# A GLU that works on feature pairs, with its 64-row remainders as two row tiles, inside a statically scheduled four-layer kernel

## The chip, the cores and the metric

One core of one Trainium2 chip. Times are microseconds (us) on the device. In this kernel TensorE does the matmuls and writes their sums to the banks of PSUM, a memory of its own; the vector engine (DVE) and the scalar engine (ACT) read them out (the evacuation), and GpSimd (POOL) does elementwise work on SBUF, the main on-chip memory. "Span" is the time from the first to the last instruction of a profiled run. In profile lines PE is TensorE's matmuls, PEld its weight loads, and L1076 is line 1076 of the kernel that ran. "A row tile" is half of the TensorE array, 64 of its 128 rows, used as an array of its own.

## The reference, cut to what matters

Two blocks A (linear attention) and two blocks B (a gated bilinear unit, GLU) alternate over 2048 tokens of width 576; each adds to x.

```
x = x + A(layernorm(x));  x = x + B(layernorm(x))      # twice

def B(x):                     # D = 576, F = 4608
    g = x @ w_gate            # [2048, 4608]
    u = x @ w_up
    return (g * u) @ w_down
```

The contraction over D = 576 is 4 chunks of 128 rows and a remainder of 64.

## The kernel before: the parts that matter

The order of instructions on each engine is fixed when the kernel is built. The kernel carries a list scheduler: each piece of work is a Python generator (a "thread") that yields groups of instructions with planned durations; the scheduler always takes the group that could start first in its plan. The GLU thread `t_bmain` has priority 10, and priority 10 has a head start ("bias") of 300 ns:

```python
SEM_LAT = 64.0                                  # planned cost of a semaphore, ns
self.bias = {10: 300.0}
...
    est = max(self.free_at[eng], tr.ready_time(deps), th.t_ready)
    key = (est - self.bias.get(int(th.prio), 0.0), -th.prio)
    if best is None or key < best[0]:
        best = (key, th, est)
```

The GLU thread, for a block b of 256 tokens and a feature tile f of 128 (cut):

```python
for i in range(total + LAG):                    # LAG = 2
    b, f = divmod(i, NF)
    if f == 0:
        yield ("wait", ("xTB", L, b))           # attention and layernorm of this block done
    gub = s.GU_BANKS[i % 2]                     # two PSUM banks alternate
    # 5 gate matmuls -> columns 0:256 of the bank, 5 up matmuls -> columns 256:512;
    # the fifth of each is the remainder, 128 rows padded with zeros
    yield ("ops", "pe", ops)
    yield ("ops", "act", [Op(372, copy gate half of the bank -> gsb)])
    yield ("ops", "dve", [Op(425, up half of the bank * gsb -> hT)])
    # then the down matmuls of tile i - LAG: 2 x (512 + 64 columns)
```

While the second half of a layer's attention still runs, its threads (projection, softmax, transposes, output projection for each of 16 token tiles) compete with the GLU thread for TensorE.

Of the kernel before, what the change touches and what calls it, by code (L numbers as in the profile page):

```python
# [424 lines left out]
def d_pe(n):  # L425
    return max(n, 64) / 2.4 + (7.0 if 288 <= n < 512 else 3.0)
# [18 lines left out]
class K:  # L445
# [19 lines left out]
    def alloc(self):  # L465
        nc = self.nc
        A = lambda name, shape, dt: self.stack.enter_context(nc.sbuf_tensor(name, shape, dt))
        self.ident = A("ident", [128, 128], BF16)
        self.onesf = A("onesf", [128, 128], F32)
        self.epst = A("epst", [128, 1], F32)  # L470
        self.mask = A("mask", [TW, TW], BF16)
        self.ind = A("ind", [TW, HT], BF16)
        self.BDphi = A("BDphi", [TW, NT, TW], BF16)
        self.BD = A("BD", [TW, 2 * NT, 114], BF16)
        self.x_sb = A("x_sb", [128, NS, D], BF16)
        self.xT = A("xT", [128, 6, S], BF16)
        self.Wq = A("Wq", [128, 4, D], BF16)
        self.Wqr = A("Wqr", [128, 288], BF16)
        self.Wk = A("Wk", [128, 4, D], BF16)
        self.Wkr = A("Wkr", [128, 288], BF16)  # L480
        self.Wv = A("Wv", [128, 4, DP], BF16)
        self.Wvr = A("Wvr", [128, 324], BF16)
        self.Wo = A("Wo", [128, 4, D], BF16)
        self.Wor = A("Wor", [128, 288], BF16)
        self.Wg = A("Wg", [128, 4, FF], BF16)
        self.Wu = A("Wu", [128, 4, FF], BF16)
        self.Wr = A("Wr", [128, FF], BF16)
        AT = lambda name, shape, dt, base: nc.alloc_sbuf_tensor_at(name, shape, dt, offset=base)
        self.NG, self.NH = 3, 4
        al32 = lambda n: (n + 31) // 32 * 32  # L490
        raw_b = al32(5 * (2 * D + 72) * 2)
        wt_b = 2 * NT * 128 * 2
        wd_b = al32(self.NWD * CH * D * 2)
        ring_b = (self.NG + self.NH) * 256 * 2
        n1 = max(raw_b + wt_b, wd_b + ring_b)
        arena1 = A("arena1", [128, n1 // 2], BF16)
        a1 = nc.lookup_mloc(arena1).addr
        self.Wraw = AT("Wraw", [128, 5, 2 * D + 72], BF16, a1)
        self.WT = AT("WT", [TW, 2, NT, 128], BF16, a1 + raw_b)
        self.wdr = AT("wdr", [128, self.NWD, CH, D], BF16, a1)  # L500
        self.gsb = AT("gsb", [128, self.NG, 256], BF16, a1 + wd_b)
        self.hT = AT("hT", [128, self.NH, 256], BF16, a1 + wd_b + self.NG * 512)
        self.xln = A("xln", [128, 2 * self.NXP, 640], BF16)
        self.st = A("st", [128, 2 * self.NXP, 12], F32)
        self.mv = A("mv", [128, 2 * self.NXP, 2], F32)
        self.lnv = A("lnv", [128, 2 * self.NXP], F32)
        self.rstd = A("rstd", [128, 2 * self.NXP], F32)
        self.nmean = A("nmean", [128, 2 * self.NXP], F32)
        self.psb = A("psb", [128, self.NPS, D], BF16)
        self.mxmn = A("mxmn", [128, self.NPS, 2, H], F32)  # L510
        self.dd = A("dd", [128, self.NSM, 2, DP], BF16)
        self.ss = A("ss", [128, self.NSM, 2 * H], F32)
        self.rr = A("rr", [128, self.NSM, 2 * H], F32)
        self.wst = A("wst", [TW, NT, DH], BF16)
        self.vx = A("vx", [128, self.NVX, NT, TW + 1], BF16)
        self.eT = A("eT", [TW, self.NET, 2 * NT, 128], BF16)
        self.den = A("den", [128, self.NET, NT * HT], F32)
        self.rden = A("rden", [128, self.NET, NT * HT], F32)
        self.o = A("o", [128, self.NET, DP], BF16)
        self.oT = A("oT", [128, self.NET, 6, 128], BF16)  # L520
        self.ps = self.stack.enter_context(nc.psum_tensor("ps", [128, 8, 512], F32))
        self.psb16 = [self.ps[:, i, :].bitcast(BF16) for i in range(8)]
        self.sbuf_left = nc.sbuf_bytes_remaining
        sc = self.sc
        sc.pool("xlnp", self.NXP)
        sc.pool("sm", self.NSM)
        sc.pool("psb", self.NPS)
        self.vx_of = {}
        self.wt_of = {}
        sc.pool("vx", self.NVX)  # L530
        sc.pool("et", self.NET)
        sc.pool("wt", 2)
        sc.pool("wd", self.NWD)
        sc.pool("pb", 3)
        sc.pool("pbx", 2)
        self.banks = {"pb": [5, 6, 7], "pbx": [3, 4]}
        self.KV_BANKS = [0, 1, 2]
        self.GU_BANKS = [0, 1]
        self.ACC0 = 2
        self.wd_slot = {}  # L540
        self.g_wd = [self.tr.dma_group("wd%d" % i) for i in range(self.NWD)]
# [502 lines left out]

    def t_bmain(self, L, on_block_done):
        s = self
        LAG = s.lag
        NG, NH = s.NG, s.NH
        ps, xT, Wg, Wu, Wr, gsb, hT = s.ps, s.xT, s.Wg, s.Wu, s.Wr, s.gsb, s.hT
        total = NB * NF  # L1050
        yield ("wait", "wloaded")
        yield ("wait", ("BD", L))
        yield ("wait", ("w", "q"))
# [1 line left out]
        x0 = x1 = None  # L1055
        pend = []
        X, Y, Z = s.ACC0, s.ACC0 + 1, s.ACC0 + 2
        for i in range(total + LAG):
            if i < total:
                b, f = divmod(i, NF)  # L1060
                if f == 0:
                    yield ("wait", ("xTB", L, b))
                gub = s.GU_BANKS[i % 2]
                tok = slice(256 * b, 256 * b + 256)
                fs = slice(128 * f, 128 * f + 128)
                rd_x = [("xT", 2 * b, 0), ("xT", 2 * b + 1, 0), ("xT", 2 * b, 1), ("xT", 2 * b + 1, 1)]
                ops = []
                for k in range(5):
                    lhsT = Wg[:, k, fs] if k < 4 else Wr[:, fs]
                    rhs = xT[:, k, tok]  # L1070
                    ops.append(Op(d_pe(256), (lambda e, lhsT=lhsT, rhs=rhs, k=k, gub=gub: e.matmul(ps[:, gub, 0:256], lhsT, rhs, start=(k == 0), stop=(k == 4))),  # L1071
                                  reads=rd_x + [("Wg",), ("Wr",)], writes=[("GUg", gub)], excl=[("pb", gub)]))
                for k in range(5):
                    lhsT = Wu[:, k, fs] if k < 4 else Wr[:, fs]
                    rhs = xT[:, k if k < 4 else 5, tok]
                    ops.append(Op(d_pe(256), (lambda e, lhsT=lhsT, rhs=rhs, k=k, gub=gub: e.matmul(ps[:, gub, 256:512], lhsT, rhs, start=(k == 0), stop=(k == 4))),  # L1076
                                  reads=rd_x + [("Wu",), ("Wr",)], writes=[("GUu", gub)], excl=[("pb", gub)]))
                yield ("ops", "pe", ops)
                g = i % NG
                h = i % NH  # L1080
                al = []
                if L == 1 and i < max(NG, NH):
                    al = [("WT", 0), ("WT", 1), ("Wraw", 1), ("Wraw", 2)] + [("Wraw", 0, w_, k_) for w_ in ("q", "k") for k_ in range(5)]
                yield ("ops", "act", [Op(372, (lambda e, g=g, gub=gub: e.copy(gsb[:, g, :], ps[:, gub, 0:256])),  # L1084
                                         reads=[("GUg", gub)], writes=[("gsb", g)] + al, excl=[("pb", gub)])])
                yield ("ops", "dve", [Op(425, (lambda e, g=g, h=h, gub=gub: e.tensor_tensor(hT[:, h, :], ps[:, gub, 256:512], gsb[:, g, :], ALU.mult)),  # L1086
                                         reads=[("GUu", gub), ("gsb", g)], writes=[("hT", h)] + al, excl=[("pb", gub)])])
            if i >= LAG:
                pend.append(i - LAG)
                b2, f2 = divmod(i - LAG, NF)  # L1090
                if f2 == 0 and b2 > 0 and i + 1 < total:
                    continue
                for j in pend:
                    b2, f2 = divmod(j, NF)
                    h2 = j % NH
                    c, fi = divmod(f2, CH)
                    if f2 == 0 and b2 > 0:
                        yield ("wait", ("x2", L, b2 - 1))
                    if x0 is None:
                        gx = yield ("acqn", ["pbx"], 2)  # L1100
                        x0, x1 = gx[0][1], gx[1][1]
                    if fi == 0:
                        yield ("wait", ("wd", L, b2, c))
                    slot = s.wd_slot[(L, b2, c)]
                    ops = []
                    for sl in range(2):
                        bank = X if sl == 0 else Y
                        lhsT = hT[:, h2, 128 * sl:128 * sl + 128]
                        ops.append(Op(d_pe(512), (lambda e, lhsT=lhsT, bank=bank, slot=slot, fi=fi, f2=f2: e.matmul(  # L1109
                            ps[:, bank, 0:512], lhsT, s.wdr[:, slot, fi, 0:512], start=(f2 == 0), stop=(f2 == NF - 1))),  # L1110
                            reads=[("hT", h2), ("wdr", slot)], writes=[("acc", sl)], excl=[("pb", bank)]))
# [6 lines left out]
                        yield ("rel", "wd", slot)  # L1118
                    if f2 == NF - 1:
                        yield ("go", s.t_bepi(L, b2, on_block_done), 8, "bepi%d" % b2)  # L1120
                pend = []
        yield ("wait", ("x2", L, NB - 1))
        yield ("rel", "pbx", x0)
        yield ("rel", "pbx", x1)
# [141 lines left out]
```

## Time and profile before

| | before |
|---|---|
| time | 1252.32 us (1251.99 to 1252.72) |
| TensorE busy | 1198.8 us of a span of 1250.4 |
| GLU of layer 1, first to last matmul start | 125.3 to 639.7 |
| attention alone between the GLUs | 92.7 us |
| GLU of layer 2 | 732.3 to 1246.1 |
| one clean pair of feature tiles | 3.16 us |

Of each GLU's 514 us, 144 pairs x 3.16 = 455 are GLU matmuls; some 59 us are attention matmuls that stand between them. This is how they stand, in the timeline of the second layer (start, duration, engine, line, count): one attention piece (L808) after the up matmuls, then the downs.

```profile
885.22 0.27 PE L1076 MATMUL ps<-xT,Wr 128*128 128x256 bf16 x1
885.33 0.65 PE L808 MATMUL ps<-Wq,xT 128*128 128x288 bf16 x4
885.82 0.29 PE L808 MATMUL ps<-Wqr,xT 128*128 128x288 bf16 x1
885.94 0.38 PE L1109 MATMUL ps<-wdr,hT 128*128 128x512 bf16 x1
```

By the start stamps of the whole trace, other work comes between GLU matmuls in 233 stretches, and 223 of them stand in this place.

### The profile page before, as it was taken

What the parts mean: (1) busy time and instruction counts of PE and PEld (TensorE: products, weight loads), DVE (VectorE), ACT (ScalarE), POOL (GpSimd) and SP (SyncE); (2) the same over time, 40 slices, a digit from 0 to 9 for tenths busy, and PEclk for the clock granted to TensorE, in tenths of its full rate; (3) what the DMA queues carried; (4) which work ended last, traced back from release to release, by engine and by line L of the source; (5) the groups of instructions that cost most, each with busy time, mean ns of one, the idle gap of its engine ahead of it and who ended that gap; (6) DMA issues with size and microseconds to landing.
All of it is one profiled execution on the core that took longest, in us unless ns stands there. A gap on an engine that the chain in (4) does not pass through costs nothing.

```text
span 1250.4 us, 25739 instructions
## 1 busy us (share of the span) xinstructions
PE 1198.8 (96%) x11096; PEld 936.1 (75%) x11096; DVE 619.3 (50%) x1478; ACT 546.4 (44%) x1393; POOL 272.5 (22%) x268
## 2 busy tenths in 40 slices
PE   6796999999999999999999889999999999999998
PEld 4574777778787777777767568778777777777776
DVE  6898646445553323323269974455445332323232
ACT  7887545445353323222258765444444322222222
POOL 4796212112120000000039742112112000000000
PEclk9998999999999999999999889999999999999999
DMA  9700122222222333333320002222222233323232
GB/s 316 230 2 1 41 75 72 74 85 72 85 73 86 88 99 89 98 90 97 94 64 2 1 2 73 86 82 74 82 84 82 86 97 99 105 91 110 87 109 67
DMA packets 85832, 104.61 MB, mean 84 GB/s; under 512 B 4374, under 2 KB 84566, under 8 KB 84566
## 3 DMA queue, kind: packets, MB, share of 16 engines
q1 hardware_dynamic: 85718, 102.96, 27.0%
q8 instruction: 87, 1.43, 0.5%
q14 instruction: 27, 0.22, 0.1%
HBM read 100.59 MB, written 2.36 MB: 82 GB/s over the span
## 4 chain that ended last, share of the span: by engine, by line
PE 84%; DVE 6%; POOL 5%; ACT 4%; issue 0%; DMA 0%; SPq 0%; DVEq 0%
PE ps L1071 25%; PE ps L1076 25%; PE ps L1109 20%; PE ps L808 4%; PE ps L1019 3%; POOL dd L869 3%; PE ps L1112 3%; DVE ss L855 2%; PE ps L946 2%; POOL dd L833 1%; PE ps L965 1%; PE ps L783 1%; DVE dd L841 1%; PE ps L998 1%; DVE mxmn L823 1%; DVE mxmn L828 1%
## 5 line engine op out<-in xcount | busy, mean ns | idle before, releaser
L1086 DVE TENSOR_TENSOR hT<-ps,gsb 128x256 bf16<-128x256 f32 x576 | 243.9, 423 | 577.2 <-ACT gsb L1084 575.9
L1084 ACT CAST gsb<-ps 128x256 bf16<-128x256 f32 x576 | 214.2, 372 | 621.7 <-PE ps L1076 585.3
L1109 PE MATMUL ps<-wdr,hT 128*128 128x512 bf16 x1152 | 357.5, 379 | 0.4 <-DVE x_sb L1135 0.4
L1071 PE MATMUL ps<-xT,Wg 128*128 128x256 bf16 x2304 | 347.2, 273 | 0.0
L1076 PE MATMUL ps<-xT,Wu 128*128 128x256 bf16 x2304 | 346.1, 273 | 0.0
L1071 PEld LDWEIGHTS ps<-xT,Wg 128*128 128x128 bf16 x2304 | 187.2, 98 | 80.8
L1076 PEld LDWEIGHTS ps<-xT,Wu 128*128 128x128 bf16 x2304 | 225.7, 98 | 26.4
L1112 PE MATMUL ps<-wdr,hT 128*128 128x64 bf16 x1152 | 221.9, 193 | 0.5 <-DVE x_sb L1138 0.5
L869 POOL TENSOR_TENSOR dd<-dd,rr 128x576 bf16<-128x576 bf16 x128 | 146.1, 1163 | 121.1 <-ACT rr L863 121.1
L1109 PEld LDWEIGHTS ps<-wdr,hT 128*128 128x128 bf16 x1152 | 112.6, 98 | 76.8 <-DVE x_sb L1135 0.7
L1071 PE MATMUL ps<-xT,Wr 128*128 128x256 bf16 x576 | 157.2, 273 | 0.0
L1076 PE MATMUL ps<-xT,Wr 128*128 128x256 bf16 x576 | 157.2, 273 | 0.0
L772 POOL TENSOR_SCALAR xln<-x_sb,nmean,rstd 128x576 bf16<-128x576 bf16 x64 | 51.9, 821 | 367.1 <-ACT rstd L767 366.9
L833 POOL TENSOR_TENSOR dd<-psb,mxmn 128x576 bf16<-128x576 bf16 x64 | 74.4, 1163 | 231.6 <-DVE mxmn L823 231.6
L1112 PEld LDWEIGHTS ps<-wdr,hT 128*128 128x128 bf16 x1152 | 112.7, 98 | 6.5 <-DVE x_sb L1138 0.8
L855 DVE TENSOR_REDUCE ss<-dd 128x64 f32<-128x1152 bf16 x64 | 86.4, 1350 | 22.8 <-ACT dd L850 22.5
L1071 PEld LDWEIGHTS ps<-xT,Wr 128*128 128x128 bf16 x576 | 56.5, 98 | 6.6
L1076 PEld LDWEIGHTS ps<-xT,Wr 128*128 128x128 bf16 x576 | 56.4, 98 | 6.6
L820 ACT CAST psb<-ps 128x288 bf16<-128x288 f32 x128 | 47.9, 400 | 17.3 <-PE ps L808 15.3
L949 ACT COPY eT<-ps 108x768 bf16<-108x768 bf16 x64 | 50.8, 798 | 8.5 <-PE ps L965 4.9
L828 DVE TENSOR_REDUCE mxmn<-ps 128x16 f32<-128x288 f32 x128 | 52.0, 448 | 0.0
L841 DVE TENSOR_TENSOR dd<-ps,mxmn 128x288 bf16<-128x288 f32 x128 | 51.7, 447 | 0.0
(85 smaller groups left out, 1143.8 us busy)
## 6 DMA issues: line engine op xcount, KB each, us to landing
wdr<-in_B_w_down_dram SPq DMA_DIRECT2D x192, 432.0 KB, 3.3
Wg<-in_B_w_gate_dram SPq DMA_DIRECT2D x4, 1152.0 KB, 12.3
Wu<-in_B_w_up_dram SPq DMA_DIRECT2D x4, 1152.0 KB, 27.3
x_sb<-in_A_x_dram SPq DMA_DIRECT2D x4, 576.0 KB, 5.8
out_dram<-x_sb SPq DMA_DIRECT2D x8, 288.0 KB, 3.7
Wraw<-in_A_wqkv_dram SPq DMA_DIRECT2D x8, 144.0 KB, 4.8
Wv<-in_A_wqkv_dram SPq DMA_DIRECT2D x1, 576.0 KB, 3.9
Wo<-in_A_wo_dram SPq DMA_DIRECT2D x1, 576.0 KB, 6.6
```

The costliest lines, as they stand in the source:

```text
L772: ops.append(Op(800, (lambda e, j=j: e.tensor_scalar(xln[:, sl[j], 0:576], x_sb[:, ss[j], :], nm[:, sl[j]:sl[j] + 1], rstd[:, sl[j]:sl[j] ...
L828: ops.append(Op(370, (lambda e, h=h, pv=pv: e.tensor_reduce(mxmn[:, pz, 1, 16 * h:16 * h + 16], pv, AX.X, ALU.min)), reads=[("pbd", bank)] ...
L833: yield ("ops", "pool", [Op(1170, (lambda e: e.tensor_tensor(d1, p3, mxb, ALU.subtract)), reads=[("psb", pz, 0), ("psb", pz, 1), ("mx", pz ...
L841: ops.append(Op(370, (lambda e, d2h=d2h, pv=pv, mnbh=mnbh: e.tensor_tensor(d2h, pv, mnbh, ALU.subtract)), reads=[("pbd", bank), ("mn", pz, ...
L855: Op(1320, (lambda e: e.tensor_reduce(ss[:, sm, :].rearrange("p (b g) -> p b g", b=2), e4, AX.X, ALU.add)), reads=s.ddk(sm, 0) + s.ddk(sm, ...
L869: yield ("ops", "pool", [Op(1150, (lambda e, ev=ev, rb=rb: e.tensor_tensor(ev, ev, rb, ALU.mult)), reads=s.ddk(sm, br) + [("rr", sm), ("dd ...
L1071: ops.append(Op(d_pe(256), (lambda e, lhsT=lhsT, rhs=rhs, k=k, gub=gub: e.matmul(ps[:, gub, 0:256], lhsT, rhs, start=(k == 0), stop=(k == ...
L1076: ops.append(Op(d_pe(256), (lambda e, lhsT=lhsT, rhs=rhs, k=k, gub=gub: e.matmul(ps[:, gub, 256:512], lhsT, rhs, start=(k == 0), stop=(k = ...
L1084: yield ("ops", "act", [Op(372, (lambda e, g=g, gub=gub: e.copy(gsb[:, g, :], ps[:, gub, 0:256])), reads=[("GUg", gub)], writes=[("gsb", g ...
L1086: yield ("ops", "dve", [Op(425, (lambda e, g=g, h=h, gub=gub: e.tensor_tensor(hT[:, h, :], ps[:, gub, 256:512], gsb[:, g, :], ALU.mult)), ...
L1109: ops.append(Op(d_pe(512), (lambda e, lhsT=lhsT, bank=bank, slot=slot, fi=fi, f2=f2: e.matmul(ps[:, bank, 0:512], lhsT, s.wdr[:, slot, fi, ...
L1112: ops.append(Op(d_pe(64) + 6, (lambda e, lhsT=lhsT, sl=sl, slot=slot, fi=fi, f2=f2: e.matmul(ps[:, Z, 64 * sl:64 * sl + 64], lhsT, s.wdr[: ...
```

## The change

Intent: the remainders of gate and up contract over 64 rows each, so a gate and an up remainder can use the two halves of the array at the same time. They are to write different PSUM banks (the prediction cites the rule), so gate gets one bank and up the other, and to fill a 512-wide bank the loop takes two feature tiles at once. The copy and the multiply become 512 wide, half as many. The core of the diff (cut):

```diff
-        self.NG, self.NH = 3, 4                       # rings of 256-wide tiles
+        self.NG, self.NH = 2, 3                       # rings of 512-wide tiles
...
-                gub = s.GU_BANKS[i % 2]
-                for k in range(5):
-                    lhsT = Wg[:, k, fs] if k < 4 else Wr[:, fs]
-                    ... ps[:, gub, 0:256], start=(k == 0), stop=(k == 4)
-                (the same for Wu into ps[:, gub, 256:512])
-                yield ("ops", "pe", ops)
+                for j in range(2):                    # the two tiles of the pair
+                    for bank, r0, kc, key in ((GB, 0, 4, "GUg"), (UB, 64, 5, "GUu")):
+                        lhsT = Wr[r0:r0 + 64, fs]
+                        rhs = xT[r0:r0 + 64, kc, tok]
+                        ops.append(Op(57 if r0 else 57, ... ps[:, bank, cs], start=(j == 0), stop=False ...))
+                ops += main(Wg, "Wg", GB, "GUg")      # 8 full-array gate matmuls
+                yield ("ops", "pe", ops)
-                yield ("ops", "act", [Op(372, copy 256 wide)])
-                yield ("ops", "dve", [Op(425, multiply 256 wide)])
+                yield ("ops", "act", [Op(590, copy 512 wide)])
+                yield ("ops", "pe", main(Wu, "Wu", UB, "GUu"))   # 8 up matmuls
+                yield ("ops", "dve", [Op(685, multiply 512 wide)])
...             (down matmuls: those of the pair before, lag of one pair)
```

## The prediction

> **What bounds the kernel now.** I read the engine table first, then the 40 slices, then the chain that ended last, then the costliest groups; last a window in the GLU stage of the second layer, where nothing else runs.
>
> ```profile
> PE 1198.8 (96%) x11096; PEld 936.1 (75%) x11096; DVE 619.3 (50%) x1478; ACT 546.4 (44%) x1393; POOL 272.5 (22%) x268
> ...
> PE   6796999999999999999999889999999999999998
> ...
> PE 84%; DVE 6%; POOL 5%; ACT 4%; issue 0%; DMA 0%; SPq 0%; DVEq 0%
> PE ps L1071 25%; PE ps L1076 25%; PE ps L1109 20%; PE ps L808 4%; PE ps L1019 3%; POOL dd L869 3%; PE ps L1112 3%; DVE ss L855 2%; PE ps L946 2%; POOL dd L833 1%; PE ps L965 1%; PE ps L783 1%; DVE dd L841 1%; PE ps L998 1%; DVE mxmn L823 1%; DVE mxmn L828 1%
> ...
> L1086 DVE TENSOR_TENSOR hT<-ps,gsb 128x256 bf16<-128x256 f32 x576 | 243.9, 423 | 577.2 <-ACT gsb L1084 575.9
> L1084 ACT CAST gsb<-ps 128x256 bf16<-128x256 f32 x576 | 214.2, 372 | 621.7 <-PE ps L1076 585.3
> ...
> L1071 PE MATMUL ps<-xT,Wr 128*128 128x256 bf16 x576 | 157.2, 273 | 0.0
> L1076 PE MATMUL ps<-xT,Wr 128*128 128x256 bf16 x576 | 157.2, 273 | 0.0
> ```
>
> TensorE fills the span, and 73% of the chain is the GLU's gate (L1071), up (L1076) and down lines (L1109, L1112). Vector and scalar engine wait for it, not it for them: the big idle figures stand in their rows, 0.0 in the matmul rows. So the change is worth what it does to TensorE's order of work in the GLU.
>
> Busy time is not the price of a matmul there: the records overlap. The timeline (start, duration, engine, line, count) gives the pitch:
>
> ```profile
> 1101.11 0.19 PE L1112 MATMUL ps<-wdr,hT 128*128 128x64 bf16 x1
> 1101.14 0.60 PE L1071 MATMUL ps<-xT,Wg 128*128 128x256 bf16 x4
> 1101.58 0.27 PE L1071 MATMUL ps<-xT,Wr 128*128 128x256 bf16 x1
> 1101.69 0.60 PE L1076 MATMUL ps<-xT,Wu 128*128 128x256 bf16 x4
> 1102.13 0.27 PE L1076 MATMUL ps<-xT,Wr 128*128 128x256 bf16 x1
> 1102.23 0.38 PE L1109 MATMUL ps<-wdr,hT 128*128 128x512 bf16 x1
> ...
> 1102.43 0.37 ACT L1084 CAST gsb<-ps 128x256 bf16<-128x256 f32 x1 [1.21 <-PE ps L1076]
> 1102.45 0.19 PE L1112 MATMUL ps<-wdr,hT 128*128 128x64 bf16 x1
> ```
>
> From 1101.14 to 1102.23 run ten 256-wide matmuls: 0.109 us each. A down matmul of 512 columns takes 0.22 (1102.23 to 1102.45), the 64-wide one after it 0.03 (1101.11 to 1101.14). One feature tile is 10 x 0.109 + 2 x 0.245 = 1.58 us; 2127 matmuls in a clean 240 us window, 14 to a tile, give 1.580 too. Two layers x 8 blocks x 36 tiles = 576 tiles are 910 us, 73% of the span. Also to be kept: the scalar engine reads the bank 0.30 us after the last up matmul STARTS, and a 256-wide record (0.273) ends 0.164 us later than its pitch.
>
> **What the Trainium skill says.** "TensorE: Matmul & The Clock Gate", Part 3 (Packing small matmuls), says that matmuls in different row groups of the array run at the same time, starting about 4 ns apart. No matmul of this kernel contracts over 64 rows, so the trace cannot confirm it. "TensorEngine Tiling (Array Packing)", Key Properties: "Changing tiling mode (not just tile) drains the TensorE"; it gives no price, and nothing before switches mode. The same page, Gotcha 1, says that different row tiles cannot write one bank at once; hence gate and up get a bank each here, where before one bank held both. The first page's Part 2 (step 4, drain) puts the array's emptying at about 128 cycles, 53 ns at 2.4 GHz; overlapped matmuls hide it, which agrees with the pitch of 0.109 us (256 columns at that clock are 0.107).
>
> **The change, part by part**, for a pair of feature tiles; there are 288.
>
> Removed: the two full-array gate remainders and the two up remainders of a pair cost 4 x 0.109 = 0.437 us; their other 64 rows were zeros or the other matrix's rows against zeros. Now the four run as two side-by-side couples, about 2 x (0.109 + 0.004) = 0.226. Saved 0.21 us a pair, 288 x 0.21 = 61 us. The count of matmuls stays 11096; this saves pitch, not instructions.
>
> Added: two mode switches a pair, from the down matmuls into 64-row tiles and back for the gate. What one costs is the question of this case. Least: the next weights cannot be pulled ahead, about 0.03 us (the 64-wide matmul shows that a load and start fit in 0.03). Most: everything in flight ends first, 0.164 us (the modelled tail of a record), plus that reload, 0.19. My estimate is the array's emptying of the skill's page, 0.053, plus part of a reload, together 0.07. Two switches are 0.14 us a pair, 288 x 0.14 = 40 us. Net of these two parts: -21 us.
>
> Changed: the scalar engine's copy and the vector engine's multiply go from 576 of 256 columns to 288 of 512. The vector engine's residual add of the same shape (128x512, one fp32 operand from PSUM) takes 0.681 us before, so 288 x 0.681 = 196 against 243.9 us. The copy, extended at the 0.875 ns a column between its 256-wide (372) and 288-wide (400) rows, is 0.596: 172 against 214.2 us. That is 90 us off two engines that do not set the end: worth nothing by itself.
>
> Moved: buffering. Before, two banks alternate, so a bank is free for 1.58 us before its next writer. Now each is rewritten by the very next pair. Gate: the copy runs under eight up matmuls (0.87) and the previous pair's downs (0.98), against 0.30 + 0.60 needed: ample. Up: the multiply starts 0.30 after the last up matmul starts, ends at 0.98, and with a wake of 0.04 TensorE may write at 1.02-1.03; its downs keep it busy until 0.109 + 4 x 0.245 = 1.09. Slack of 0.06 us: it just fits, as long as the vector engine takes the multiply at once and downs lie between.
>
> They don't at two places. At the start of a block the first pair's downs are held back until the residual adds are done, so one pair's remainders follow the previous pair's up matmuls at once: 1.03 - 0.11 = 0.92 us of stall at 7 block changes a layer, 13 us, of which I leave 7, as attention work fills some in the first half of a layer. And while attention still runs, the multiply can queue behind vector work of up to 1.35 us (L855); some 24 attention tiles run inside the two GLUs, at perhaps 0.3 us each: 7 us. Together +14 us.
>
> Sum: 1252 - 61 + 40 + 14 = 1245; I say 1244.
>
> **The rivals.**
> (1) A switch costs the whole tail, 0.19 us. Then a pair pays 0.38 to save 0.21: +49 us, and somewhat less of the vector stalls, since they hide under the switch (+10): about 1310. For it: "drains the TensorE" may mean just that, and the kernel before pads its remainders to 128 rows with zeros at real cost, as if someone had found 64-row matmuls dear. Against: a pair gathers all four remainders behind one switch each way, a lot of work for a loss.
> (2) A switch is nearly free, 0.03 or less: -61 + 17, and the stalls +17, since the 0.06 us of slack is all there is: about 1225; at zero cost 1210.
> (3) The single up bank becomes the bound: vector engine late by a few tenths of a microsecond in most of the roughly 120 pairs that run beside attention, some 30 us instead of 7: about 1268. For it: vector busy is 54% there (53.81 in the slice 200 to 300); against: the order of instructions puts attention matmuls between.
> (4) The couples do not overlap (issued in order, the second waiting on its bank): nothing saved, switches paid: 1252 + 40 + 14 = 1306.
> A transfer does not come into it: the down weights are read as before, at 0.32 DMA share.
>
> **Range and chances.** The time is nearly linear in the price of a switch, 5.8 us for each 0.01 us. Below 0.04 us it is faster by over 2% (under 1227); from 0.04 to about 0.125 it is within 2%; above that slower. I give 0.33, 0.38 and 0.29, with rivals 3 and 4 in the upper part. The range 1205 to 1300 holds a nearly free switch and reaches to one of about 0.17 us.
>
> **What would show it.** In a clean window of the second layer: pair period near 3.09 us (3.16 before); the two starts of a couple within 0.03 us, couples 0.11 apart; from the last 64-wide down matmul to the first remainder 0.1 us instead of 0.03, and the same from the last remainder (its own 0.11 apart) to the first gate matmul. Multiply near 681 ns, x288; copy near 596. TensorE idle behind the multiply: near 0.9 us at block changes, little elsewhere. I am wrong if a switch shows over 0.12 or under 0.04 us, if couples start 0.11 apart, or if waits of the remainders for the multiply add up to over 25 us.

## The result, and the profile after

The changed kernel takes 1383.98 us (1383.31 to 1385.59) against 1252.15 for the kernel before in the same rounds: ratio 1.1054, 95% interval 1.1039 to 1.107. Ratios here are the mean time of one kernel's runs over that of the other's in the same rounds, so not quite the ratio of the medians quoted. It is slower by 132 us; I had said 1244 and given 1300 as the upper end.

The page of the changed kernel (engine table, then TensorE's busy tenths and granted clock in 40 slices, then two groups):

```profile
PE 1238.5 (90%) x10952; PEld 869.2 (63%) x11096; DVE 584.5 (42%) x1190; ACT 505.6 (37%) x1105; POOL 272.5 (20%) x268
...
PE   6887999997988989897997789999979898999998
...
PEclk9998999998999999898999999999989999998999
...
L1100 DVE TENSOR_TENSOR hT<-ps,gsb 128x512 bf16<-128x512 f32 x288 | 199.1, 691 | 650.1 <-PE ps L1085 647.4
L1097 ACT CAST gsb<-ps 128x512 bf16<-128x512 f32 x288 | 168.8, 586 | 682.0 <-PE ps L1085 681.7
```

No other engine has become busier. TensorE has: 39.7 us more busy time for the same 11096 matmuls (144 records are missing in this trace), and 92.2 us more in which it is not busy (1382.3 - 1238.5 = 143.8 against 51.6; some 8 us of that are holes that the missing records leave). The slices that were solid 9s now have 7s and 8s in a regular beat, with dips of the clock beside them. First the clean part, a pair in the second layer:

```profile
1301.08 0.19 PE L1128 MATMUL ps<-wdr,hT 128*128 128x64 bf16 x1
1301.20 0.39 PE L1073 MATMUL ps<-xT,Wr 64*128 64x256 bf16 x4
1301.53 1.05 PE L1085 MATMUL ps<-xT,Wg 128*128 128x256 bf16 x8
1302.41 1.04 PE L1085 MATMUL ps<-xT,Wu 128*128 128x256 bf16 x8
1303.29 0.38 PE L1125 MATMUL ps<-wdr,hT 128*128 128x512 bf16 x1
...
1304.36 0.39 PE L1073 MATMUL ps<-xT,Wr 64*128 64x256 bf16 x4
```

From 1301.20 to 1304.36: 3.16 us, exactly the pair of the kernel before. The four remainders do run as two couples: the four records span 0.39 us, one of them lasts 0.277, so the last starts 0.11 after the first, not three times 0.109. But 0.12 us pass before them (a 64-wide matmul needs 0.03) and 0.33 from their start to the first gate matmul (two steps of 0.11 would be 0.22). So in the clean part the change is a draw, and the 132 us are elsewhere.

They are at the block starts. There the timeline shows long stretches without one GLU matmul. Twelve of over 4 us lie within the two GLUs after their first blocks; the kernel before has none there. Four of them and the sum of all twelve, in the windows view (window, its length, busy time and count of each engine, granted TensorE clock, DMA share, GB/s):

```profile
core 0: us, PE busy (x) PEld busy (x) DVE busy (x) ACT busy (x) POOL busy (x), PEclk, DMA share, GB/s
...
320.30:343.90 23.60, 13.62 (x108) 8.82 (x106) 13.50 (x31) 13.49 (x32) 7.75 (x8) 0.80 0.07 20
...
636.80:649.20 12.40, 5.10 (x51) 3.30 (x50) 4.24 (x13) 5.28 (x13) 1.63 (x2) 0.71 0.12 36
...
1003.00:1031.00 28.00, 18.62 (x156) 13.39 (x155) 15.22 (x38) 15.20 (x32) 8.47 (x8) 0.76 0.05 16
...
1236.80:1259.10 22.30, 16.14 (x130) 11.84 (x130) 11.38 (x31) 11.47 (x24) 5.08 (x5) 0.71 0.07 21
sum 194.70, PE 123.78 PEld 87.71 DVE 102.81 ACT 106.95 POOL 40.56; mean PE 10.32 PEld 7.31 DVE 8.57 ACT 8.91 POOL 3.38
```

In no engine's column does busy time reach the length of the window: nobody is full, each waits for the next in a chain. And the clock is down to 0.71 to 0.80 in these four (0.81 to 1.00 in the other eight). What runs in one of them:

```profile
1003.04 0.19 PE L1128 MATMUL ps<-wdr,hT 128*128 128x64 bf16 x1
1003.07 0.44 PE L998 MATMUL ps<-ident,o 128*128 128x128 bf16 x5
...
1004.58 0.66 PE L1019 MATMUL ps<-Wo,oT 128*128 128x288 bf16 x4
...
1007.19 0.66 PE L1019 MATMUL ps<-Wo,oT 128*128 128x288 bf16 x4 [1.82 <-DVE x_sb L1023]
...
1015.21 0.71 PE L998 MATMUL ps<-ident,o 128*128 128x128 bf16 x5 [1.03 <-DVE o L987]
...
1016.99 1.14 PE L1019 MATMUL ps<-Wo,oT 128*128 128x288 bf16 x4 [0.43 <-ACT oT L1004]
```

Attention, and only attention: output projection, transposes, softmax of the two token tiles that the next GLU block needs, step by step, each waiting in brackets for DVE or ACT. At 1016.99 the same group of four L1019 matmuls takes 1.14 us in place of 0.66. The granted clock of the whole window is 0.76, and the windows view gives 0.50 from 1013.9 to 1020.7: the clock falls in the holes and adds to the loss. In the kernel before such work stood between up and down and left no hole: from 200 to 600 us TensorE was busy for all of the 400 us.

The books: the GLU of layer 1 (first to last matmul start, 125.8 to 709.5) takes 583.7 us, 69.3 more; the stretch between the GLUs 105.3, 12.6 more; the GLU of layer 2 (814.8 to 1378.0) 563.2, 49.4 more. Together 131 of the 132 us.

### The profile page after: what moved, and what is told of

The parts are those of the page before. It is cut to its first block, busy times and chain, and to the rows that moved or that the text cites. A ratio compares the mean times of both kernels' runs of the same rounds, so it can differ in the third digit from the quotient of the medians.

```text
span 1382.3 us, 25273 instructions
## 1 busy us (share of the span) xinstructions
PE 1238.5 (90%) x10952; PEld 869.2 (63%) x11096; DVE 584.5 (42%) x1190; ACT 505.6 (37%) x1105; POOL 272.5 (20%) x268
## 4 chain that ended last, share of the span: by engine, by line
PE 77%; DVE 9%; ACT 9%; POOL 2%; issue 2%; DMA 0%; SPq 0%; DVEq 0%
PE ps L1085 39%; PE ps L1125 16%; PE ps L1073 7%; PE ps L1128 4%; PE ps L808 3%; PE ps L1019 3%; DVE ss L855 2%; ACT xT L788 2%; POOL dd L869 2%; ACT eT L949 2%; PE ps L783 1%; PE ps L946 1%; DVE o L987 1%; DVE st L751 1%; DVE mxmn L828 1%
## 5 line engine op out<-in xcount | busy, mean ns | idle before, releaser
L1100 DVE TENSOR_TENSOR hT<-ps,gsb 128x512 bf16<-128x512 f32 x288 | 199.1, 691 | 650.1 <-PE ps L1085 647.4
L1097 ACT CAST gsb<-ps 128x512 bf16<-128x512 f32 x288 | 168.8, 586 | 682.0 <-PE ps L1085 681.7
L1085 PE MATMUL ps<-xT,Wg 128*128 128x256 bf16 x2304 | 306.3, 277 | 0.0
L1085 PE MATMUL ps<-xT,Wu 128*128 128x256 bf16 x2304 | 302.9, 275 | 0.0
L1125 PE MATMUL ps<-wdr,hT 128*128 128x512 bf16 x1008 | 284.1, 380 | 0.0
L1073 PE MATMUL ps<-xT,Wr 64*128 64x256 bf16 x1152 | 116.0, 277 | 13.7 <-ACT xT L790 11.7
L1073 PEld LDWEIGHTS ps<-xT,Wr 64*128 64x128 bf16 x1152 | 33.6, 94 | 82.9 <-issue 63.0
L1019 PE MATMUL ps<-Wo,oT 128*128 128x288 bf16 x256 | 53.2, 342 | 15.5 <-ACT oT L1004 9.8
L788 ACT COPY xT<-ps 128x640 bf16<-128x640 bf16 x64 | 44.3, 692 | 33.0 <-PE ps L783 27.7
L823 DVE TENSOR_REDUCE mxmn<-psb 128x32 f32<-128x576 bf16 x64 | 47.7, 745 | 20.4 <-ACT psb L820 19.9
```

The lines of the kernel that those rows point to most:

```text
L788: Op(d_act(640, True), (lambda e, pT=pT, tok=tok: e.copy(xT[:, 0:5, tok], pT[:, 0:640].rearrange("p (k n) -> p k n", k=5))), reads=[("pbd" ...
L1019: ops.append(Op(d_pe(288), (lambda e, lhsT=lhsT, rhs=rhs, k=k, bank=bank: e.matmul(s.ps[:, bank, 0:288], lhsT, rhs, start=(k == 0), stop=( ...
L1073: ops.append(Op(57 if r0 else 57, (lambda e, lhsT=lhsT, rhs=rhs, bank=bank, cs=cs, j=j: e.matmul(ps[:, bank, cs], lhsT, rhs, start=(j == 0 ...
L1085: o_.append(Op(d_pe(256), (lambda e, lhsT=lhsT, rhs=rhs, k=k, bank=bank, cs=cs: e.matmul(ps[:, bank, cs], lhsT, rhs, start=False, stop=(k ...
L1097: yield ("ops", "act", [Op(590, (lambda e, g=g: e.copy(gsb[:, g, :], ps[:, GB, :])), reads=[("GUg",)], writes=[("gsb", g)] + al, excl=[("p ...
L1100: yield ("ops", "dve", [Op(685, (lambda e, g=g, h=h: e.tensor_tensor(hT[:, h, :], ps[:, UB, :], gsb[:, g, :], ALU.mult)), reads=[("GUu",), ...
```

## Theories, and the experiments

**Theory 1, the lost turn.** In the kernel before, the multiply waits for the copy, the copy for the up matmuls (gate and up share a bank, and the plan lets a reader into a bank only when all that was written to it earlier is done: `excl=[("pb", gub)]`). In the scheduler's plan the multiply can start 64 + 372 + 64 = 500 ns after the up matmuls end; less the head start of 300 that is +200. An attention matmul that is ready when the up matmuls end stands at 0 and goes first; only then come the multiply and the downs. In the changed kernel the copy is planned under the 877 ns of up matmuls, so the multiply is ready 64 ns after they end; less 300 that is -236, and the GLU's matmul groups stand at -300. Attention's turn hardly ever comes until the GLU thread blocks at the next block start, waiting for just that attention. The loss comes from the order of instructions, not from the array.

**Theory 2**, my rival (3) of the prediction: the banks, no longer alternating, make TensorE wait for the vector engine.

**Theory 3**: the mode switches of the row tiles.

Trace evidence so far is against 2: all waits of the remainders for the multiply (L1073 behind hT L1100) sum to 1.9 us in the changed kernel. All twelve kernels below gave correct results.

**1. The changed kernel, head start 0.**

```diff
-        self.bias = {10: 300.0}
+        self.bias = {10: 0.0}
```

> The changed kernel with one number altered: the head start that the kernel's own list scheduler gives the GLU thread goes from 300 ns to 0. Theory 1 (the attention tiles' matmuls no longer get a place between the GLU's up and down, so they run alone, latency-bound, at the block starts): attention is spread through the GLU again and the time falls from 1384 to 1250-1275, near the kernel before, because a clean pair takes 3.16 us in both. Theory 2 (the single gate and up banks make TensorE wait for the vector engine): stays within 20 us of 1384. Theory 3 (the mode switches of the 64-row tiles cost it): stays at 1384 too.

1261.81 us, ratio to before 1.0077 (1.006 to 1.0094). 122 of the 132 us are gone, with the same banks, tiles and evacuations. Theories 2 and 3 are left with 10 us net. The page shows the full row again. Attention is back inside the GLU, though not all in its old place: of 237 stretches of other work 106 stand between up and downs and 120 between gate and up. The waits show what the single bank does cost (engine, line, whom it waited for; total, times, longest):

```profile
PE 1201.0 (95%) x11096; PEld 853.2 (68%) x11096; DVE 581.5 (46%) x1190; ACT 499.1 (40%) x1105; POOL 272.1 (22%) x268
...
PE   6796999999999999999999789999999999999998
```

```profile
PE ps L1073 <- DVE hT L1100: 7.1, 10, 1.0
```

**2. The kernel before, head start 600.** Nothing of the change is in it.

```diff
-        self.bias = {10: 300.0}
+        self.bias = {10: 600.0}
```

> The kernel before with one number altered: the GLU thread's head start is 600 ns in place of 300, more than the 200 ns by which the multiply, waiting for the copy, loses its turn. No pairs, no 64-row tiles, two alternating banks. Theory 1: attention is starved here too, the time rises from 1252 to 1350-1385, with the same holes at block starts. Theories 2 and 3: within 10 us of 1252, since neither the banks nor the tiles are touched.

1421.76 us, ratio 1.1351 (1.1334 to 1.1367), mean clock 0.938. One number makes the old kernel slower than the change did, with the same picture:

```profile
PE   6887999997989998798988789999989798979888
...
PEclk9998999997999999799999899999989799999989
```

The direction is as theory 1 says; the size is 37 us above my range, so I understood that attention is starved but not how much each hole costs.

**3. The changed kernel with full 128-row remainders** (one after the other, no mode switch).

```diff
-                        lhsT = Wr[r0:r0 + 64, fs]
-                        rhs = xT[r0:r0 + 64, kc, tok]
+                        lhsT = Wr[:, fs]
+                        rhs = xT[:, kc, tok]
```

> The changed kernel, but the four remainders of a pair are full 128-row matmuls again (the zero-padded operands of the kernel before), so no mode switch and nothing side by side; pairs, single banks and 512-wide evacuations stay. Clean pair: 4 x 0.109 + 0.02 in place of the 0.45 us that stands in the changed kernel from the last down matmul to the first gate matmul, so 3.16 us again. Theory 1: 1365-1395, about as slow as the change. Theory 3: back to about 1252. Theory 2: as theory 1, within 20 us of 1384.

1405.0 us, ratio 1.1218 (1.1195 to 1.1241): 10 us above the range, and slower than with tiles. Theory 3 falls: without a switch anywhere the loss is all there. A clean pair takes 3.16 to 3.17 us. The tiles seem worth 21 us in the starved order and 4 in the other (next run). Some 17 of the 21 are in the holes, which fall differently: the stretches of over 4 us without a GLU matmul inside the two GLUs sum to 222 us here and to 206 in the changed kernel.

**4. The same, head start 0** (edits 1 and 3 together).

> Both: pairs with full 128-row remainders, and a head start of 0. Theory 1: 1255-1275; set beside the run of the changed kernel with head start 0 it prices the 64-row tiles alone: if two switches eat just what running side by side saves, the two are within 10 us. Theory 2: stays near 1384 as the banks are still single.

1265.96 us, ratio 1.0106 (1.0091 to 1.0121). Against run 1 the tiles are worth 4 us in 1262. The edit also changes the remainders' planned duration, and so the order; a difference this small is not the tiles' alone for certain.

**5. What one mode switch costs.** The kernel before, its gate remainder alone on 64 rows.

```diff
-                    lhsT = Wg[:, k, fs] if k < 4 else Wr[:, fs]
-                    rhs = xT[:, k, tok]
+                    lhsT = Wg[:, k, fs] if k < 4 else Wr[0:64, fs]
+                    rhs = xT[:, k, tok] if k < 4 else xT[0:64, 4, tok]
```

> The kernel before with one edit: the gate remainder contracts over its own 64 rows instead of 128 zero-padded ones, alone, in its old place. Same instructions, same order, same banks; two mode switches in each of 576 feature tiles. In the changed kernel a switch seems to add 0.10 us (last down matmul to first remainder 0.125 in place of 0.027, last couple to first gate matmul 0.21 in place of 0.109). If that is the price of a switch: 576 x 0.20 = +115 us, 1350-1385. If the gaps there were waits for the vector engine or for the couples: within 20 us of 1252.

1373.51 us, ratio 1.096 (1.0946 to 1.0975): 120.6 us for 1152 switches, 0.105 us each. The timeline shows both gaps of a tile:

```profile
1301.06 0.60 PE L1071 MATMUL ps<-xT,Wg 128*128 128x256 bf16 x4
1301.59 0.28 PE L1071 MATMUL ps<-xT,Wr 64*128 64x256 bf16 x1
1301.80 0.61 PE L1076 MATMUL ps<-xT,Wu 128*128 128x256 bf16 x4
1302.25 0.27 PE L1076 MATMUL ps<-xT,Wr 128*128 128x256 bf16 x1
```

Four gate matmuls at 0.109 should bring the remainder at 1301.50; it starts at 1301.59. By the start stamps of all 576 tiles the median step into the 64-row matmul is 205 ns and the step out 212, where the kernel before has 109 and 109: 96 and 103 ns. So the zero padding pays in that kernel: a padded matmul (0.109) is cheaper than two switches (0.20). How a switch's time divides between emptying the array and loading weights that could not be pulled ahead, the runs don't tell.

**6. Remainders in the middle, head start 0.** The four remainders go between the gate and the up matmuls of their pair, so the up bank has to be free 0.9 us later.

```diff
-                ops += main(Wg, "Wg", GB, "GUg")
-                yield ("ops", "pe", ops)
+                rem = ops
+                yield ("ops", "pe", main(Wg, "Wg", GB, "GUg", True) + rem)   # start flag on the first gate matmul
```

> The changed kernel with head start 0, and the four remainders moved from the start of a pair to between its gate and up matmuls, so the up bank is first written 0.9 us later. If the 0.10 us ahead of the remainders was a wait for the multiply, it goes and the time falls by 288 x 0.10 = 29 us to about 1233; if it is the mode switch it stays, in the new place. In either case the 7.1 us of stalls behind the multiply at block starts should go: 1252-1258 against 1262.

1255.52 us, ratio 1.0014 (0.9999 to 1.0029); no wait for the multiply is left in the trace. So the stalls at block starts were real and worth about 6 us (8 by the two ratios; the order changed too), and the gap ahead of the remainders is not a wait for the vector engine, for it moved with them:

```profile
1101.49 1.04 PE L1087 MATMUL ps<-xT,Wg 128*128 128x256 bf16 x8
1102.46 0.39 PE L1073 MATMUL ps<-xT,Wr 64*128 64x256 bf16 x4
1102.78 1.05 PE L1087 MATMUL ps<-xT,Wu 128*128 128x256 bf16 x8
```

Eight gate matmuls end their turn at 1101.49 + 8 x 0.109 = 1102.36; the remainders start 0.10 later.

**7. The same, head start 50.**

```diff
-        self.bias = {10: 0.0}
+        self.bias = {10: 50.0}
```

> As the one before with a head start of 50 ns, under the 64 ns that the scheduler allows for a semaphore, so attention still gets its turn between up and down, but fewer turns elsewhere. Theory 1: as fast as with 0 or up to 10 us faster, 1245-1258; no return to 1384.

1248.4 us, ratio 0.9962 (0.9949 to 0.9974): the fastest kernel, 0.4% under the one before.

**8. The same, with the switches in the plan.**

```diff
+                rem[0].dur += 95
...
+                um[0].dur += 110                      # the first up matmul
```

> As the one before, and the scheduler is told what the switches cost (95 ns on the first remainder, 110 ns on the first up matmul), so that its order fits the chip better. The clean pair cannot change (3.16 us); 1245-1258, at most 5 us from the one before.

1251.87 us, ratio 0.9989 (0.9976 to 1.0002). An honest plan was not better; 3.5 us worse. No cause was looked for; differences of this size between two orders stay unexplained here.

**9. Only the plan of the changed kernel altered.** This goes to the narrow point of theory 1: head start 300 as in the change, and the copy merely planned as slow.

```diff
-                yield ("ops", "act", [Op(590, (lambda e, g=g: e.copy(gsb[:, g, :], ps[:, GB, :])),
+                yield ("ops", "act", [Op(1400, (lambda e, g=g: e.copy(gsb[:, g, :], ps[:, GB, :])),
```

> The changed kernel with the head start left at 300 ns. Only the duration that the scheduler plans for the gate copy goes from 590 to 1400 ns; the instruction itself is the same. The planned multiply then becomes ready 0.65 us after the up matmuls in place of 0.06, beyond the head start, so attention gets its turn again, as in the kernel before (0.50 us there). Theory 1, in its narrow form (the turn was lost because the multiply no longer waits for the copy): 1255-1280. If the head start works in another way: near 1384.

1259.2 us, ratio 1.005 (1.0033 to 1.0067). A false figure in the plan takes back 125 us, and attention is back in its old place: 176 of 188 stretches of other work stand between up and downs, where the changed kernel has 4 of 33.

**10. The mirror image in the kernel before.**

```diff
-                yield ("ops", "act", [Op(372, ...copy...
+                yield ("ops", "act", [Op(60, ...copy...
```

> The mirror image: the kernel before, head start 300, with the planned duration of its copy cut from 372 to 60 ns, so that its multiply is planned 0.19 us after the up matmuls, inside the head start. Same instructions, two banks, no tiles. Narrow theory 1: starved, 1390-1425, like the kernel before with head start 600. Otherwise 1252.

1399.27 us, ratio 1.1162 (1.1137 to 1.1187). The old kernel loses 146 us when the plan says that the multiply need not wait.

**11. The fastest version without tiles** (edit 3 in run 7).

> The fastest version so far (remainders in the middle, head start 50) with full 128-row remainders: the tiles alone are undone. If running side by side pays for its two switches and leaves 0.01-0.02 us a pair: 3-10 us slower than the version with tiles, 1252-1260.

1253.27 us, ratio 1.0012 (0.9994 to 1.003): 4.9 us slower than run 7, or 6 by the ratios (the two ran on different chips). Tiles against full rows is 4 to 6 us in both undisturbed comparisons, each with its own order; the start stamps below give 4.9.

**12. The kernel before, head start 400.**

> The kernel before with a head start of 400 ns, still under the 500 ns at which its multiply is planned. Theory 1: no starving, 1245-1256; a rise of over 20 us would say that the threshold lies elsewhere. It also tells whether the 0.4% of the fastest version is within reach of the scheduler's number alone.

1251.85 us, ratio 0.9984 (0.9968 to 1.0001). Between 400 (planned multiply 100 ns too late for its head start) and 600 (100 ns early) lies the cliff of 170 us, where theory 1 puts it, at 500. The interval of this run overlaps that of run 7, so it isn't shown that the 0.4% of run 7 needs the tiles.

| kernel | multiply planned after up, less head start | time, us |
|---|---|---|
| before, 300 | +200 | 1252 |
| before, 400 | +100 | 1252 |
| before, 600 | -100 | 1422 |
| before, copy planned 60 | 188 - 300 = -112 | 1399 |
| change, 300 | -236 | 1384 |
| change, full rows, 300 | -236 | 1405 |
| change, 0 | +64 | 1262 |
| change, copy planned 1400 | 651 - 300 = +351 | 1259 |
| remainders in the middle, 50 | +14 | 1248 |

Every positive row is fast and every negative one slow, whatever the tiles and banks. Of the runs left out, 4, 6, 8 and 11 (+64, +64, +14, +14) are fast too; run 5 (+200) is slow by its 1152 switches. The traces agree: the four kernels with a negative row have 13 to 16 stretches of over 4 us without a GLU matmul inside the two GLUs, 206 to 228 us together; every other kernel has at most two, of 12 us together. As runs 9 and 10 altered one planned duration and no instruction, that settles the cause of the 132 us.

## Why the prediction was wrong, point by point

- **What bounds the kernel** was right: TensorE's order of work in the GLU.
- **Saved by the couples**: right. The two starts of a couple are 3 ns apart, and the next couple starts 116 ns after the second of them (median start stamps), so two couples take 3 + 116 + 3 + 109 = 231 ns where I had 226.
- **Price of a switch**: mis-sized. I took 0.07 us from 53 ns of emptying plus part of a reload; it is 93 to 105 ns. The whole passage from the last down matmul to the first gate matmul is 125 + 3 + 116 + 3 + 202 = 449 ns against 466 with full rows (median of run 4). The gain of a pair is 17 ns in place of 70: 4.9 us in all (runs 4 and 11: 4.2 and 4.9) where I had 21. This alone would have put the time within 2%.
- **Evacuations**: right in every figure: multiply 691 ns (I said 681), copy 586 (596), x288, and off the path.
- **Single banks**: right. Run 1 has 7.1 us of waits behind the multiply, up to 1.0 each, in 10 places, eight of them the third pair of a block; I had 7 us at block starts, from 0.92 each. Of the other 7 us, which I laid on vector work in the overlap, two waits of 0.7 us together show. Rival 3 is refuted.
- **The step that failed**: "against: the order of instructions puts attention matmuls between", and with it the silent assumption of the whole sum that attention would keep its place in the GLU. I treated the instruction order as given. It is computed, from the very dependence that the change removes: multiply on copy, copy on the last up matmul. I had quoted the idle lines of DVE and ACT that show this chain, and read them as time that costs nothing. In the plan that wait was attention's place. The change took it away: 4 stretches of other work are left between up and downs in place of 223, the rest runs in the holes at block starts, and the order alone is worth 122 to 125 of the 132 us (runs 1 and 9). Put the order back (run 1) and the measured terms give 1253 - 5 + 7 = 1255 against 1262. The 7 us between them were not traced; in run 8 the plan alone moved the time by 3.5 us.
- **Rivals and range**: none of the four named a change of order of other threads, so the upper end of 1300 was set by rivals of the GLU alone.

Partly open: why a starved order costs 132, 146, 152 or 168 us (the change, runs 10, 3 and 2). The stretches without a GLU matmul rank the same way, 206, 217, 222 and 228 us; what sets their length in each kernel I did not trace. Open: why the stretch between the GLUs grows by 12.6 us. It does so in all four starved kernels (105 to 110 us) and in no other (89 to 94), so it belongs to the order too.

## What to carry to other kernels

When a kernel's instruction order comes from a scheduler, read a change in two ways: what the engines do with it, and what the scheduler does with it; a dependence that is removed may be the one that let other work in. Look for it in the trace as the place where foreign instructions stand, and ask which planned wait made that place. Row tiles pay only when they save more than two mode switches: here four remainders behind one pair of switches just broke even.

## What the Trainium skill lacked or had wrong

- "TensorEngine Tiling (Array Packing)", Key Properties, says that changing the mode drains TensorE and gives no price. Here a switch costs 96 to 98 ns going into 64-row tiles and 93 to 103 coming out (start stamps), 0.105 us by the time of 1152 switches. Two switches cost about as much as two 256-wide matmuls.
- "TensorE: Matmul & The Clock Gate", Part 3, puts about 4 ns between the matmuls of neighbouring row tiles: confirmed, 3 ns. It has nothing on the next couple: that starts 116 ns after the second matmul of the first, where full-array matmuls of this width step by 109.
- The same page, "Why this matters for your kernels", warns of TensorE gaps of over about 3 us. Shorter ones can be enough: in the hole from 1003 to 1031 us the longest wait of TensorE was 1.9 us and it was busy for 18.6 of 28 us, yet the granted clock there was 0.76. The page's section "A second HAM failure mode: psum-queue depth-cycling" (HAM is its name for the block that gates the clock) does say that frequent short idles of TensorE make the clock swing; what it lacks is how much idleness does it. Here TensorE was busy for 1.25 of the 3.4 us before the clock fell to 0.50.
